# Exponentials in units of three and two PSUM banks, in a kernel whose instruction order a planner writes

## The chip, the core and the metric

The kernel runs on one core of one Trainium2 chip. The metric is the device time of one execution in microseconds; the times shown are of three runs, and the profile is of one further execution on the same chip type.

## What is computed

`x` is 2048 tokens of 512 bf16 values. Block A is attention with 32 heads of 16, block B is an MLP mixer, and a gate mixes both:

```python
def _A_ref(x, wqkv, wo):                    # S = 2048, D = 512, H = 32 heads, Dh = 16
    q, k, v = split(x @ wqkv)
    p = softmax(q @ k.T * Dh ** -0.5)       # 32 x 2048 x 2048 scores
    return (p @ v) @ wo
def _B_ref(x, w1, w2, w3, w4):
    h = gelu(layernorm(x) @ w1)
    hs = shift_quarters(h) @ w2             # quarters of D move by 1, -1, 2, -2 tokens
    x1 = x + hs
    return x1 + gelu(layernorm(x1) @ w3) @ w4      # w3: 512 x 1792
g = sigmoid((x * gate_w).sum(-1))
out = g * _A_ref(x, ...) + (1 - g) * _B_ref(x, ...)
```

The exponentials of 32 x 2048 x 2048 scores are by far the most elements: 2048 tiles of 128 keys by 512 queries (16 blocks of keys, 4 chunks of queries, 32 heads).

## The kernel before

**Rounds and tiles.** Attention goes in 32 rounds (`rounds`): a chunk c of 512 queries, a group G of eight heads, and a parity p that picks four heads of it. A round has 64 score tiles: 16 key blocks (`kt`) times four heads (`i`). One score matmul (`qk_op`, L1313) contracts the 16 values of a head, in a 32-row strip of TensorE, so four heads can run side by side. Queries of the other parity are zeroed by masks `mE` and `mO` (`q_proj`, L1038 and L1040). Each tile fills one PSUM bank of 512 fp32 columns, of which there are eight.

**Two engines make exponentials.** ScalarE takes a unit of `w` tiles in `w` neighbouring banks with one ACTIVATE (`issue_act`, L1408). VectorE takes single tiles by arithmetic on the bits (`issue_dve`, L1439); for each pair of these, VectorE and GpSimd make three shifted copies (L1482, L1484), so that a VectorE tile costs four PV matmuls (L1537) where a ScalarE tile costs one. The results lie in 40 slots of the tile `prob`.

**Column work.** PV matmuls add up in one bank per round (`accs`), 32 output rows of a head each. All projections (Q, K, V, the MLP's four, the output projection) are objects of the class `Gen`: units of four matmuls, one per 32-column strip, that share one bank; VectorE then empties the bank (`evac`). They run through the helper at L964. TensorE changes between score batches (row strips) and column work all the time.

**A planner writes the order.** At build time the class `Sim` models the five engines with fixed durations; `pe_pick` decides at each moment what TensorE does next: first ScalarE units, then VectorE tiles with them, then column work up to the time when a ScalarE unit is expected to end. The result is one fixed instruction order for each queue; SyncE issues nearly all DMAs in one order. What the planner may do is set by the table `BASE`, changed every eight tiles by `STEPS`. What matters here:

- `CAP2` and `CAP3`: the most banks that ScalarE's units may hold when a unit of two or three is added. Before, `CAP3=0` forbids threes until step 253 of 256 (eight tiles a step).
- `GATE`: a ScalarE unit is only started while ScalarE holds at most so many banks.
- `LIMD`, `LIMA`: how many banks VectorE's tiles and projections (`others()`) may hold.
- `DVE_STOP`, `DVE_WAIT`, `DVE_ALONE`, `GP2`, `GP3`, `MAXU`: when VectorE takes tiles, who makes the copies, and how much column work goes in one piece.

```python
            for w, cap in ((3, K.CAP3), (2, K.CAP2)):
                if act_banks[0] + w > cap or free < w + K.RES or not sim.fits(Run("bank", w)):
                    continue
```

**Start and end.** The first two chunks of x are transposed on TensorE (`x_transposes`, L996) and copied out by ScalarE and VectorE (L1006); K of head group 0 for chunk 0 is copied by ScalarE (L1019). After the last PV matmul, the last round's division and output projection follow (L1890 to L1939); `LG` says how many head groups of the last chunk's output projection are added before that.

Of the kernel before, what the change touches and what calls it, by code (L numbers as in the profile page):

```python
# [127 lines left out]
class Gen:  # L128
# [325 lines left out]
def kernel(  # L454
# [14 lines left out]
    nc = tc.nc  # L469
# [12 lines left out]
    LG = 2  # L482
# [45 lines left out]
        ROT=2, DUE_SH=-14, AT_SH=0, HOLE=7, MAXG=1, CAP2=6, CAP3=0, LIMD=3, RES=0, GATE=2, E_PRIO=2, AFIRST=0, AGE=12000, ROWM=99, ACC2=0, LIMA=3, JOIN=0,  # L528
# [3 lines left out]
        0: dict(P1_PRIO=0.743, PV_IDLE=0.5, LIMD=4, E_PRIO=0.25),  # L532
        1: dict(P1_PRIO=0.414, GP2=0.655, PV_IDLE=0.731, MAXU=7, E_PRIO=2, AGE=20000, ROWM=7),
        3: dict(URG=11),
        4: dict(GP2=1, PRESS=43),
        5: dict(DVE_STOP=8),
        6: dict(B_LOW=1),
        8: dict(PV_FULL=0.813, PRESS=26, E_PRIO=0.4),
        9: dict(PV_FULL=0.916),
        11: dict(PV_FULL=0.813, MAXU=2),  # L540
        12: dict(HOLE=2),
        13: dict(S_PRIO=0.178),
        14: dict(AFIRST=1),
        15: dict(SL0=130, HOLE=7),
        16: dict(ROT=3),
        17: dict(URG=3, ROWM=99),
        18: dict(SL0=60),
        21: dict(EARLY=64, B_LOW=5),
        22: dict(DVE_STOP_L=16, ROT=0),
        23: dict(DVE_STOP_L=14, EARLY=99, B_LOW=1, ROT=3),  # L550
        24: dict(AT_SH=69),
        25: dict(PV_FULL=0.916, DUE_SH=-6),
        26: dict(DVE_STOP=13, DVE_WAIT=4, PRESS=15),
        27: dict(P1_PRIO=0.312),
        28: dict(JOIN=1),
        29: dict(AT_SH=34),
        31: dict(E_PRIO=2),
        32: dict(DVE_STOP=8),
        33: dict(P1_PRIO=0.55, GP3=0.9, DVE_STOP=13, DUE_SH=-14, E_PRIO=0.4),
        35: dict(AGE=12000),  # L560
        36: dict(URG=11),
        37: dict(GP2=0.8),
        39: dict(AHEAD=16),
        41: dict(PV_FULL=0.86, PV_IDLE=0.5),
        42: dict(P1_PRIO=0.312),
        43: dict(DVE_STOP=6),
        44: dict(CAP2=5),
        45: dict(B_LOW=0, HOLE=2),
        46: dict(GP3=0.8, ROWM=7),
        47: dict(SL0=-150, AFIRST=0),  # L570
        48: dict(S_PRIO=0.214, SL1=-150),
        49: dict(PRESS=11),
        50: dict(SL1=0, B_LOW=3),
        51: dict(DVE_ALONE=138),
        53: dict(DVE_STOP_L=16, PV_FULL=0.947),
        54: dict(P1_PRIO=0.414, GP2=0.315, GP3=1, DVE_STOP=4, DVE_STOP_L=14, URG=3, DVE_ALONE=500, SL0=45, SL1=-75,
            BRES=2, DVE_WAIT=3, AHEAD=24, AHEAD2=24, PV_IDLE=0.117, PRESS=18, MAXU=9, ROT=0, AT_SH=0, HOLE=3, CAP2=6,
            E_PRIO=2, AFIRST=2, ROWM=99, JOIN=0),
        55: dict(DVE_ALONE=2),
        56: dict(GP2=1, DVE_STOP=13),  # L580
        58: dict(S_PRIO=0.625, AHEAD=16, ROWM=5),
        59: dict(DVE_STOP=6),
        61: dict(SL0=60),
        62: dict(AT_SH=69, AGE=20000),
        63: dict(EARLY=64, BRES=0, HOLE=7),
        64: dict(DVE_STOP=4, PV_IDLE=0.5),
        65: dict(SL0=0),
        66: dict(DVE_WAIT=1),
        67: dict(P1_PRIO=0.136, AT_SH=96, HOLE=2),
        68: dict(P1_PRIO=0.312),  # L590
        69: dict(URG=2, ROT=3),
        70: dict(AGE=12000),
        71: dict(PV_FULL=0.916),
        73: dict(DVE_STOP=8),
        75: dict(DVE_WAIT=2),
        77: dict(S_PRIO=0.214, HOLE=0),
        78: dict(PV_FULL=0.86),
        79: dict(URG=11),
        80: dict(P1_PRIO=0.136),
        81: dict(S_PRIO=0.625),  # L600
        82: dict(AHEAD=5, HOLE=7, ACC2=1),
        83: dict(HOLE=2),
        84: dict(PV_FULL=0.947, ROT=2),
        85: dict(P1_PRIO=0.743, URG_L=18),
        87: dict(ROT=0),
        88: dict(AHEAD=24),
        89: dict(URG=8, AT_SH=69),
        93: dict(S_PRIO=0.178),
        94: dict(GP3=0.8, PV_FULL=0.916, MAXG=2),
        95: dict(DVE_STOP_L=7, ROT=3),  # L610
        97: dict(CAP2=5, AGE=6000),
        98: dict(SL1=0),
        99: dict(ROT=0),
        100: dict(ROT=3),
        101: dict(PV_FULL=0.86, MAXU=5, ROT=0, AT_SH=34, ROWM=99),
        102: dict(S_PRIO=0.625, DVE_WAIT=4, PRESS=11, AGE=3000),
        104: dict(AFIRST=1),
        106: dict(DVE_ALONE=500, AGE=20000, ROWM=5),
        108: dict(ROT=2, LIMA=4),
        109: dict(GP2=0, ROT=3),  # L620
        110: dict(S_PRIO=0.178, URG=2),
        111: dict(GP3=1, AFIRST=0),
        112: dict(P1_PRIO=0.279, S_PRIO=0.214, GP2=1, GP3=0.9, DVE_STOP=4, DVE_STOP_L=16, URG=11, URG_L=12, DVE_ALONE=2,
            EARLY=99, SL0=60, IDLE_NS=374, DVE_WAIT=3, AHEAD=7, PV_FULL=0.947, PV_IDLE=0.117, PRESS=15, MAXU=3, ROT=0,
            DUE_SH=0, AT_SH=0, HOLE=0, MAXG=1, LIMD=3, GATE=4, ROWM=99, ACC2=0, LIMA=3),
        113: dict(P1_PRIO=0.55, S_PRIO=0.178, PV_FULL=0.916),
        114: dict(HOLE=2),
        116: dict(URG=8, DUE_SH=16, MAXG=2),
        117: dict(IDLE_NS=459, B_LOW=8, ACC2=1),
        118: dict(P1_PRIO=0.279, S_PRIO=0.214, URG=11, DVE_ALONE=500, IDLE_NS=374, B_LOW=3, AHEAD=9, PV_FULL=0.947,  # L630
            ROT=1, DUE_SH=0, AT_SH=118, HOLE=7, MAXG=1, ROWM=7, ACC2=0),
        119: dict(PV_FULL=0.813),
        120: dict(DVE_STOP=6, DVE_WAIT=2),
        121: dict(AGE=12000),
        122: dict(GP2=0.315, GP3=1, EARLY=64),
        123: dict(GP2=0.15, PRESS=26),
        124: dict(DVE_STOP=4, DVE_ALONE=-158, EARLY=99, SL0=-75, IDLE_NS=537, DVE_WAIT=3, PV_FULL=0.947, PV_IDLE=0.5,
            PRESS=18, DUE_SH=-9, AT_SH=34, LIMD=4, AGE=20000),
        125: dict(GP2=0),
        126: dict(DVE_STOP_L=12, DUE_SH=0),  # L640
        127: dict(LIMD=3),
        128: dict(DVE_WAIT=4, DUE_SH=-14, ROWM=3),
        129: dict(GP2=0.15),
        130: dict(GP3=0.9, LIMA=2),
        131: dict(MAXU=7, ROWM=7),
        136: dict(P1_PRIO=0.55, URG=5),
        139: dict(P1_PRIO=0.279, URG=11),
        140: dict(ROT=0),
        141: dict(P1_PRIO=0.55, URG=5, ROT=3, AGE=3000, LIMA=3),
        144: dict(P1_PRIO=0.279, URG=11, ROT=1, AGE=20000, LIMA=2),  # L650
        146: dict(URG=2),
        147: dict(PV_FULL=0.86),
        148: dict(ROT=3),
        150: dict(GP3=0.967, URG=11, PV_FULL=0.947, ROT=1),
        151: dict(GP3=0.9, URG=2),
        152: dict(IDLE_NS=374, E_PRIO=0.25, AGE=3000),
        153: dict(GP3=1),
        154: dict(DVE_STOP_L=7, SL1=60, IDLE_NS=700),
        155: dict(PV_FULL=0.86, PRESS=43),
        156: dict(E_PRIO=0.1),  # L660
        158: dict(ROWM=3),
        161: dict(URG=3, ROWM=5),
        163: dict(PV_IDLE=0.731, AGE=12000, LIMA=4),
        164: dict(IDLE_NS=459, PRESS=15, MAXG=2),
        165: dict(S_PRIO=0.178, DUE_SH=0, ACC2=1),
        167: dict(ROT=3),
        168: dict(HOLE=3),
        171: dict(SL1=-75),
        173: dict(HOLE=0),
        174: dict(GP3=0.9),  # L670
        175: dict(P1_PRIO=0.414, S_PRIO=0.38, GP2=1, DVE_STOP=8, DVE_STOP_L=16, URG=8, URG_L=18, DVE_ALONE=2, SL0=0,
            SL1=0, IDLE_NS=537, DVE_WAIT=3, PV_FULL=0.813, PV_IDLE=0.117, PRESS=26, MAXU=5, ROT=1, DUE_SH=-9, AT_SH=96,
            HOLE=7, MAXG=1, CAP2=6, GATE=2, E_PRIO=2, AGE=20000, ROWM=3, ACC2=0, LIMA=2),
        176: dict(URG=11, AT_SH=34, AGE=6000),
        177: dict(ROT=0),
        178: dict(ROT=1),
        179: dict(LIMD=4, E_PRIO=0.4),
        181: dict(ROT=2),
        182: dict(GP3=0.8, MAXU=4),
        183: dict(GP3=0.9, MAXU=5, ROT=1),  # L680
        186: dict(DVE_STOP=6, EARLY=64, AHEAD2=16),
        187: dict(SL1=60, MAXG=2, ACC2=1),
# [1286 lines left out]
```

## Time and profile before

| what | value |
|---|---|
| runs | 756.38, 755.15, 756.24 us, median 756.24 |
| profiled execution | 755.0 us, span 753.0 us, granted clock 0.998 |
| busy: PE, DVE, ACT, POOL | 738.9, 685.8, 732.4, 458.2 us |
| ScalarE exponentials (L1408) | 746 of two banks, 1 of three |
| VectorE exponentials (L1439) | 549 of one bank, 2 of two |
| score matmuls (L1313), PV matmuls (L1537) | 2048, 3707 |
| first exponential starts, last one ends | 10.3 us, 743.9 us after the span's start |

Busy time is the union of an engine's instructions. ScalarE's and TensorE's instructions overlap in the records, so the mean duration of one is longer than the step from one to the next. "PEld" is TensorE's weight load, which runs ahead of the matmul and shows what the matmul waited for.

### The profile page before, as it was taken

How to read it: one execution, taken by the hardware profiler on the slowest of the kernel's cores; microseconds unless marked ns; L12 is line 12 of the kernel's file. 1: busy time of each engine (PE TensorE's matmuls, PEld its weight loads, DVE VectorE, ACT ScalarE, POOL GpSimd, SP SyncE). 2: the span in 40 equal slices, each digit the busy share in tenths (PEclk: the TensorE clock that was granted, in tenths of full speed). 3: DMA queues.
4: the chain of work that ended last, by engine and by line, in shares of the span. 5: the costliest groups of instructions: out<-in, count | busy, mean ns of one | idle time of the engine just before them, and what ended most of it. 6: DMA issues, size and time to landing. Idle time of an engine off the chain costs nothing.

```text
span 753.0 us, 23698 instructions
## 1 busy us (share of the span) xinstructions
PE 738.9 (98%) x9520; PEld 213.2 (28%) x9520; DVE 685.8 (91%) x1422; ACT 732.4 (97%) x768; POOL 458.2 (61%) x456
## 2 busy tenths in 40 slices
PE   8999999999999999998999999999999999999997
PEld 4324322223222222222322222222222223222222
DVE  5999999998999999997999999998989999887897
ACT  6999999999999999998999999999999999999995
POOL 2274686657866676665544545557657877774542
PEclk9999999999999999999999999999999999999999
DMA  9403331221123220025001100012000000101001
GB/s 199 143 4 79 68 85 33 66 66 44 57 61 73 69 55 21 21 72 114 8 24 27 38 26 24 10 30 52 21 20 18 20 6 27 28 24 28 20 7 46
DMA packets 67093, 34.59 MB, mean 46 GB/s; under 512 B 46748, under 2 KB 62380, under 8 KB 66984
## 3 DMA queue, kind: packets, MB, share of 16 engines
q1 hardware_dynamic: 66040, 32.56, 17.0%
q8 instruction: 74, 1.21, 0.7%
q10 hardware_dynamic: 944, 0.52, 0.2%
q14 instruction: 35, 0.29, 0.1%
HBM read 17.40 MB, written 6.81 MB: 32 GB/s over the span
## 4 chain that ended last, share of the span: by engine, by line
PE 85%; DVE 5%; ACT 4%; DMA 4%; issue 1%; POOL 0%; SPq 0%; DVEq 0%; POOLq 0%; ACTq 0%
PE banks L1537 30%; PE banks L1313 29%; PE banks L964 24%; ACT prob L1408 3%; DMA pk<-den 2%; DVE prob L1439 2%; DVE prob L1482 1%; DMA den<-accsb 1%; ACT hT L1218 1%; PE banks L943 0%; DVE st L1122 0%; PE banks L1890 0%; DMA zE_dram<-ot 0%; POOL prob L1484 0%; DMA xnT<-xn_dram 0%
## 5 line engine op out<-in xcount | busy, mean ns | idle before, releaser
L1408 ACT ACTIVATE prob<-banks 128x1024 bf16<-128x1024 f32 (+1 forms) x747 | 687.7, 1143 | 6.3 <-PE banks L1313 5.2
L1484 POOL TENSOR_SCALAR prob<-prob 128x1024 uint16<-128x1024 uint16 x394 | 405.7, 1048 | 255.4 <-DVE prob L1482 108.7
L1439 DVE TENSOR_SCALAR prob<-banks 128x512 uint16<-128x512 f32 x551 | 364.0, 683 | 29.6 <-PE banks L1313 25.6
L1537 PE MATMUL banks<-prob,V 128*17 128x512 bf16 (+1 forms) x3707 | 318.3, 382 | 1.3 <-POOL prob L1484 0.6
L1313 PE MATMUL banks<-q,kT 32*128 32x512 bf16 x2048 | 283.2, 385 | 2.8 <-ACT prob L1408 0.9
L1482 DVE TENSOR_SCALAR prob<-prob 128x1024 uint16<-128x1024 uint16 (+1 forms) x437 | 172.6, 440 | 5.8 <-PE banks L1537 1.7
L1313 PEld LDWEIGHTS <-kT 32*128 32x128 bf16 x2048 | 70.9, 91 | 306.5 <-ACT prob L1408 277.2
L1537 PEld LDWEIGHTS <-V 128*17 128x17 bf16 (+1 forms) x3707 | 71.4, 88 | 122.4 <-issue 102.2
L964 PE MATMUL banks<-xnT,w 128*32 128x512 bf16 x1152 | 91.1, 384 | 3.4 <-DMA xnT<-xn_dram 3.4
L964 PE MATMUL banks<-w,hT 128*32 128x512 bf16 x692 | 63.2, 383 | 0.0
L964 PEld LDWEIGHTS <-w 128*32 128x32 bf16 x1920 | 39.7, 95 | 53.3 <-issue 31.4
L1576 POOL TENSOR_TENSOR oT<-accsb,bcs 128x512 bf16<-128x512 f32 x31 | 39.5, 1275 | 21.0 <-DVE prob L1482 8.4
L964 PE MATMUL banks<-w,hB 128*32 128x512 bf16 x448 | 40.0, 382 | 0.0
L964 PE MATMUL banks<-w,w 128*32 128x256 bf16 (+1 forms) x768 | 38.7, 311 | 0.6 <-DVE V L1063 0.4
L975 PE MATMUL banks<-wo,oD 32*128 32x512 bf16 x72 | 27.7, 384 | 0.0
L1211 DVE CAST hT<-banks 128x512 bf16<-128x512 f32 x28 | 19.1, 682 | 5.2 <-PE banks L964 5.2
L1211 DVE CAST hB<-banks 128x512 bf16<-128x512 f32 x28 | 19.0, 682 | 4.6 <-PE banks L964 4.5
L1558 DVE COPY accsb<-banks 128x512 f32<-128x512 f32 x31 | 21.1, 680 | 1.8 <-PE banks L1537 1.7
L964 PE MATMUL banks<-w,wq 128*32 128x512 bf16 x256 | 21.5, 390 | 0.7 <-ACT w L1006 0.7
L964 PEld LDWEIGHTS <-hT 128*32 128x32 bf16 x692 | 15.9, 95 | 20.3 <-issue 13.7
L1122 DVE BATCH_NORM_STATS2 st<-x_sb 128x6 f32<-128x512 bf16 x32 | 21.1, 678 | 0.0
L964 PE MATMUL banks<-wo,oD 128*32 128x512 bf16 x152 | 20.1, 384 | 0.1
(94 smaller groups left out, 259.1 us busy)
## 6 DMA issues: line engine op xcount, KB each, us to landing
bcs<-rr SPq DMA_DIRECT2D x124, 64.0 KB
xn_dram<-xn SPq DMA_DIRECT2D x32, 128.0 KB
w<-in_B_w_dram SPq DMA_DIRECT2D x5, 512.0 KB
oD<-oT SPq DMA_DIRECT2D x124, 16.0 KB
w<-in_B_w_dram SPq DMA_DIRECT2D x4, 448.0 KB
out_dram<-ot SPq DMA_DIRECT2D x14, 128.0 KB
x_sb<-in_A_x_dram SPq DMA_DIRECT2D x3, 512.0 KB
w<-in_A_wqkv_dram SPq DMA_DIRECT2D x2, 256.0 KB
```

The costliest lines, as they stand in the source:

```text
L964: units.append([Op("col", j, lambda j=j, lf=lf, rf=rf, n0=n0, n1=n1, st=st, sp=sp: nc.tensor.matmul(get()[32 * j:32 * j + 32, n0:n1], lhsT ...
L975: o = Op("row", i, lambda: nc.tensor.matmul(get(), lhsT=lf(0, P)[rows], rhs=rf()[rows], start=False, stop=True, tile_position=(32 * i, 0), ...
L1122: a = dve(600, deps, lambda: nc.vector.bn_stats(out=sb.slot[:], in_=x_sb[:, t, :]), prio=6, at=at, acq=[sb])
L1211: pre.append(evac(g, PSUM_NS, lambda ps, m=m: nc.vector.tensor_copy(out=h2()[:, m, :], in_=ps[:])))
L1313: o = Op("row", i, lambda: nc.tensor.matmul(dst(), lhsT=kT[G][32 * i:32 * i + 32, kt * P:(kt + 1) * P], rhs=qbuf[G, c].slot[32 * i:32 * i ...
L1408: job = act(hold, ops, lambda: nc.scalar.activation(out=prob[:, pb.cut(), :].bitcast(BF16), in_=unit()[:, rb.cut(), :], func=ACT.Exp, scal ...
L1439: return nc.vector.tensor_scalar(out=prob[:, b0.cut() if w == 2 else b0.bufs[h0].slot, :], in0=unit()[:, rb.cut() if w == 2 else rb.bufs[0 ...
L1482: return nc.vector.tensor_scalar(out=cut(k), in0=cut(0), scalar1=float(SHIFT * k), scalar2=None, op0=ALU.add)
L1484: return nc.gpsimd.tensor_scalar(out=cut(k), in0=cut(0 if both else 2), scalar1=1.0, scalar2=float(SHIFT * (k if both else 1)), op0=ALU.mu ...
L1537: return nc.tensor.matmul(one(accs[r])[32 * i:32 * i + n, :], lhsT=lhs(n), rhs=rhs(), start=st and not edge, stop=True, tile_position=(0, ...
L1558: e = dve(PSUM_NS, round_ops[r], lambda: nc.vector.tensor_copy(out=ab.slot[:], in_=one(accs[r])), acq=[ab], prio=0, frees=[accs[r], Call(a ...
L1576: n = gp(1250, d3, lambda: nc.gpsimd.tensor_tensor(out=ob.slot[:], in0=ab.slot[:], in1=bb.slot[:], op=ALU.mult), acq=[ob], frees=[ab, bb], ...
```

## The change

ScalarE's units may have three banks from the start: `CAP3=5`, and `CAP2` goes from 6 to 5, so ScalarE holds five banks at most, and a unit of three is tried ahead of one of two. `GATE` is 4, 2, 3 or 9 by stages. The whole table `STEPS` is replaced. Besides:

- A projection's input buffers are given back by the matmul that is issued last, not by the one whose strip completes the last unit.
- Chunk 0 is transposed block by block, each in a bank of its own; K of group 0 for chunk 0 is made in two halves (`k_first`), and tiles of its first two key blocks may start after the first half; the first masked queries are written half by VectorE, half by ScalarE; chunk 1's transposes and V's projection wait for that (`begun`), and chunk 1's copies are all VectorE's.
- The planner's durations are changed (ns): loads of transposed x from 3100 to 3500, writes of `xn_dram` from 2200 to 2600, loads of `xnT` from 3000 to 3600, of `pk` from 2000 to 2800, of `bcs` from 2200 to 3000; around a Gelu 3050 becomes 3450 in the first layer and 2750 in the second.
- `LG` is 3 rather than 2; at the end the fp32 additions (`add_y`) come first, and the output projection of the known groups may start earlier if its inputs are expected in time.

```diff
@@ Gen.take
-        if min(self.cp) == self.cp[j]:
-            for x in self.units[k]:
-                if x is not o:
-                    o.frees += x.frees
-                    x.frees = []
+        rest = [i for i in range(4) if self.cp[i] < self.cp[j]]
+        if rest:
+            self.units[k][rest[-1]].frees += o.frees
+            o.frees = []
@@ settings
-    LG = 2
+    LG = 3
-        ROT=2, DUE_SH=-14, AT_SH=0, HOLE=7, MAXG=1, CAP2=6, CAP3=0, LIMD=3, RES=0, GATE=2, E_PRIO=2, AFIRST=0, AGE=12000, ROWM=99, ACC2=0, LIMA=3, JOIN=0,
+        ROT=2, DUE_SH=-14, AT_SH=0, HOLE=7, MAXG=1, CAP2=5, CAP3=5, LIMD=3, RES=0, GATE=2, E_PRIO=2, AFIRST=0, AGE=9000, ROWM=99, ACC2=0, LIMA=3, JOIN=0,
     STEPS = {
-        0: dict(P1_PRIO=0.743, PV_IDLE=0.5, LIMD=4, E_PRIO=0.25),
-        1: dict(P1_PRIO=0.414, GP2=0.655, PV_IDLE=0.731, MAXU=7, E_PRIO=2, AGE=20000, ROWM=7),
...
+        0: dict(GP2=1, URG=8, B_LOW=8, DVE_WAIT=1, PV_IDLE=0.5, GATE=4, AFIRST=2),
+        1: dict(SL1=130, AT_SH=34),
...
+        28: dict(DVE_WAIT=2),
+        30: dict(DVE_WAIT=1, PRESS=18, GATE=3),
...
+        41: dict(MAXU=2, GATE=9, LIMA=4),
...
+        62: dict(DUE_SH=-9, GATE=3, LIMA=2),
...
+        249: dict(GP2=0.15, DUE_SH=16, GATE=9),
@@ x_transposes: one call for each block of chunk 0
-    x_transposes(0, 0, j_x0)
-    x_transposes(0, 1, j_x0)
-    k_proj(0, 0, -1)
+    for k in range(KT):
+        x_transposes(0, (k,), j_x0)
+    k_first()
     q_proj(0, 0, -1)
-    x_transposes(1, 0, j_x1)
-    x_transposes(1, 1, j_x1)
+    begun = [j_ka[0], j_q[0, 0, 0]]
+    x_transposes(1, (0, 2), j_x1 + begun)
+    x_transposes(1, (1, 3), j_x1 + begun)
@@ who copies the transposed blocks
-            j_xT[c, 0, k] = (dve if k % 2 else act)(340 if k % 2 else 500, g.units[k // 2], cp, prio=0, frees=[g.buf])
+            on_dve = c or k % 2
+            j_xT[c, 0, k] = (dve if on_dve else act)(375 if on_dve else 535, g.units[n], cp, prio=0, frees=[g.buf])
@@ new
+    def k_first():
+        for h in range(2):
+            g = gen("k0", -1, [j_xT[0, 0, k] for k in range(KT)] + [dl_w["k0"]],
+                    [(lambda a, b, k=k: W("k")[:, k, a:b],
+                      lambda k=k, h=h: W("x00")[:, k, 256 * h:256 * h + 256], 0, 256, k == 0, k == KT - 1, 107.5)
+                     for k in range(KT)], due=-3 + h)
+            if h:
+                g.ops[-1].frees += [wb["k"], wb["x00"]]
+            j = act(275, g.units[-1], lambda g=g, h=h: nc.scalar.copy(out=kT[0][:, 256 * h:256 * h + 256],
+                                                                      in_=one(g.buf)[:, 0:256]), prio=0, frees=[g.buf])
+            if h:
+                j_k[0, 0] = j
+            else:
+                j_ka.append(j)
@@ q_proj, first block only
-            e1 = dve(680, g.units[-1] + [j_m3], lambda: nc.vector.tensor_scalar(
-                out=qb.slot[:, 0, :], in0=one(g.buf)[:], scalar1=mE[:], scalar2=None, op0=ALU.mult), prio=0, acq=[qb])
+            e1 = [dve(345, g.units[-1] + [j_m3], lambda: nc.vector.tensor_scalar(
+                out=qb.slot[:, 0, 0:256], in0=one(g.buf)[:, 0:256], scalar1=mE[:], scalar2=None, op0=ALU.mult), prio=0,
+                acq=[qb])]
+            e1.append(act(330, g.units[-1] + [j_m3], lambda: nc.scalar.activation(
+                out=qb.slot[:, 0, 256:512], in_=one(g.buf)[:, 256:512], func=ACT.Copy, scale=mE[:]), prio=0))
@@ tile_ok
+        k = j_ka[0] if G == 0 and kt < 2 else j_k.get((G, kt // 4))
@@ room
-        return sim.free["bank"] and others() < K.LIMD
+        return sim.free["bank"] and others() < (K.LIMD if sim.tiles else NBANK)
@@ end
-    early = (0, 1) if max(d.done for d in packs) < tl - 500.0 else ()
+    early = (0, 1) if max(d.done for d in packs) < tl + 1500.0 else ()
...
-    for tt in range(4):
-        if tt not in early:
-            known(tt, range(LG, 3))
-    add_y(1)
-    add_y(3)
+    for tt in (1, 3):
+        add_y(tt, tt not in early)
     for tt in range(4):
         if tt not in early:
-            known(tt, (3,))
+            known(tt, range(LG, 4), tt % 2 == 0)
```

More of the change, by code (lines that the diff above doesn't have):

```diff
@@ new lines @@
+        1: dict(SL1=130, AT_SH=34),
+        2: dict(DUE_SH=-9),
+        3: dict(SL0=130),
+        4: dict(AHEAD=5, AT_SH=69),
+        6: dict(URG=3),
+        7: dict(SL1=60),
+        8: dict(S_PRIO=0.178, PRESS=57),
+        9: dict(E_PRIO=0.1),
+        10: dict(P1_PRIO=0.279),
+        11: dict(P1_PRIO=0.414),
+        13: dict(P1_PRIO=0.136),
+        14: dict(URG=8, PV_FULL=0.97),
+        16: dict(GP3=0.8, IDLE_NS=864, AGE=20000),
+        21: dict(MAXU=3),
+        22: dict(URG_L=18, AT_SH=118),
@@ new lines @@
+        68: dict(ROT=2),
+        70: dict(ROT=3, AFIRST=2, LIMA=2, JOIN=0),
+        71: dict(GP3=1),
+        74: dict(URG=11),
+        75: dict(GP3=0.8, URG=2),
+        76: dict(AT_SH=96),
+        77: dict(URG=5, AHEAD=12),
+        78: dict(URG=3),
+        83: dict(DVE_STOP=6),
+        84: dict(B_LOW=3, ROT=0),
+        85: dict(GP3=1),
+        86: dict(GP3=0.8),
+        88: dict(AT_SH=34),
+        89: dict(P1_PRIO=0.414, GP2=0.315, ACC2=0),
+        90: dict(P1_PRIO=0.136, GP2=0.15, DVE_ALONE=500, PRESS=26, ACC2=1),
@@ new lines @@
+        93: dict(DVE_STOP=8, URG=8),
+        94: dict(PV_FULL=0.813, PV_IDLE=0.5),
+        95: dict(DVE_STOP=6, URG=3, PV_FULL=0.97, PV_IDLE=0.117, PRESS=8),
+        96: dict(GP3=0.967),
+        98: dict(SL0=-75, AGE=12000),
+        100: dict(SL1=-150),
+        101: dict(SL1=-75, IDLE_NS=374, HOLE=2),
+        102: dict(AFIRST=0),
+        103: dict(MAXU=4),
+        104: dict(MAXU=5),
+        105: dict(SL0=-150),
+        106: dict(GP3=0.8, LIMA=4),
+        107: dict(URG_L=12, MAXU=2),
@@ new lines @@
+        108: dict(URG_L=18, MAXU=5),
+        109: dict(ACC2=0),
+        111: dict(URG_L=12, MAXU=2, ACC2=1),
+        112: dict(BRES=4, AHEAD=7, PRESS=15, JOIN=1),
+        114: dict(GP2=0.315),
+        115: dict(SL1=0, BRES=0),
+        116: dict(GP2=1, URG=2, EARLY=99),
+        118: dict(GP2=0.655),
+        119: dict(SL1=130),
+        120: dict(GP2=0.15, DVE_STOP_L=12, MAXU=7),
+        121: dict(SL0=0, AT_SH=118),
+        122: dict(HOLE=0, JOIN=0),
+        124: dict(B_LOW=5, ROT=2, AGE=3000),
@@ new lines @@
+        125: dict(PRESS=26),
+        126: dict(HOLE=7),
+        128: dict(DVE_STOP=8, PV_FULL=0.813),
+        129: dict(GP3=0.967, EARLY=64, IDLE_NS=459),
+        130: dict(GP3=0.8, ROWM=3),
+        132: dict(PRESS=18),
+        133: dict(PV_FULL=0.947, DUE_SH=-14),
+        134: dict(GP3=0.633),
+        135: dict(GP3=0.8),
+        136: dict(ROWM=99),
+        137: dict(GP3=0.9, AHEAD2=16, ACC2=0),
+        138: dict(AHEAD=24),
+        142: dict(GP2=0.8),
+        143: dict(GP3=1, PRESS=11),
@@ new lines @@
+        146: dict(AGE=12000),
+        147: dict(GP3=0.9, PRESS=18, AGE=3000),
+        150: dict(GP2=1, ACC2=1),
+        152: dict(GP2=0.8, ACC2=0),
+        153: dict(HOLE=0),
+        154: dict(S_PRIO=0.3, DVE_STOP_L=14),
+        155: dict(S_PRIO=0.178, DVE_STOP_L=12),
+        156: dict(ROWM=7),
+        157: dict(HOLE=7),
+        158: dict(P1_PRIO=0.743, GP3=0.967, B_LOW=0, DVE_WAIT=3),
+        159: dict(P1_PRIO=0.136, DVE_STOP=6, URG=3),
+        162: dict(DVE_WAIT=1, ROWM=3),
+        166: dict(AFIRST=2),
@@ new lines @@
+        185: dict(ROT=3),
+        186: dict(SL1=130, ROT=2, AT_SH=69, E_PRIO=2),
+        187: dict(SL1=60, DVE_WAIT=4, ROT=3, AT_SH=0, E_PRIO=0.1),
+        188: dict(P1_PRIO=0.414, DVE_STOP=13, B_LOW=2, MAXG=1),
+        189: dict(MAXU=3),
+        191: dict(AGE=20000, ACC2=1),
+        192: dict(DVE_STOP=6),
+        193: dict(ROT=1),
+        194: dict(ROT=3),
+        195: dict(PRESS=26),
+        196: dict(PRESS=18, ROT=1),
+        197: dict(DVE_STOP=8, PRESS=43),
+        198: dict(DVE_STOP=6, URG=8, PRESS=18),
@@ new lines @@
+        200: dict(DVE_STOP=4),
+        201: dict(URG_L=18, AHEAD=3, AFIRST=0),
+        202: dict(DVE_ALONE=362),
+        203: dict(GP2=0),
+        204: dict(P1_PRIO=0.279),
+        205: dict(P1_PRIO=0.414, GP2=0.8, DVE_ALONE=500, ROWM=7),
+        208: dict(P1_PRIO=0.136),
+        209: dict(SL0=0, HOLE=3),
+        210: dict(AT_SH=69),
+        212: dict(GP2=0.15),
+        213: dict(HOLE=0),
+        214: dict(AGE=3000),
+        215: dict(AGE=20000),
+        216: dict(SL0=130, B_LOW=0),
@@ new lines @@
+        218: dict(SL0=0, B_LOW=2, AGE=3000),
+        219: dict(GP3=0.9, IDLE_NS=374),
+        220: dict(AT_SH=0),
+        221: dict(GP3=0.967, ROT=3),
+        223: dict(GP2=0.8, URG_L=12, AGE=12000),
+        224: dict(SL0=-75, AGE=6000),
+        228: dict(AGE=3000),
+        230: dict(ACC2=0),
+        231: dict(DVE_STOP_L=16, SL1=130, PV_FULL=0.86),
+        232: dict(P1_PRIO=0.279),
+        234: dict(GP3=0.9),
+        235: dict(URG=5, B_LOW=3),
+        238: dict(URG=8, DVE_ALONE=362, B_LOW=1),
@@ L905, in load_xT @@
     def load_xT(c, k, part, prio):
-        return dma(3100.0, [], lambda: xT_dma(c, part, k)(nc.sync), hold=1280.0, prio=prio,
+        return dma(3500.0, [], lambda: xT_dma(c, part, k)(nc.sync), hold=1280.0, prio=prio,
                    acq=[wb[f"x{c}{part}"]] if k == 0 else [])
@@ L1016, in k_proj @@
         g.ops[-1].frees += [wb["k"], wb[f"x{c}0"]]
-        if G == 0 and c == 0:
-            g.due = -3
-            j_k[G, c] = act(500, g.units[-1], lambda: nc.scalar.copy(out=kT[G][:, 0:512], in_=one(g.buf)[:]), prio=0,
-                            frees=[g.buf])
-            return
-        g.due = 14 * c - 6 if G == 0 else g.due
+        g.due = 14 * c - 11 if G == 0 else g.due
         j_k[G, c] = evac(g, PSUM_NS, lambda ps: nc.vector.tensor_copy(out=kT[G][:, c * 512:(c + 1) * 512], in_=ps[:]),
@@ L1057, in v_proj @@
         c = u // 2
-        g = gen("v", at, [j_xT[c, 0, k] for k in range(KT)] + [dl_w[f"v{hh}"]],
+        g = gen("v", at, begun + [j_xT[c, 0, k] for k in range(KT)] + [dl_w[f"v{hh}"]],
                 [(lambda a, b, t=t, k=k: W(f"x{c}0")[:, k, (t % 4) * P + a:(t % 4) * P + b],
@@ L1151, in normalise @@
         for k in range(KT):
[L1152 removed]
+            js.append(dma(3600.0, ds, hold=1280.0, fn=lambda k=k: nc.sync.dma_start(
                 out=tb.slot[:, k, :], in_=xn_dram[which, c * 512:(c + 1) * 512, k * P:(k + 1) * P], transpose=True),
@@ L1307, in tile_ok @@
         c, G, p = rounds[r]
-        return ready_round(r) and j_k.get((G, kt // 4)) is not None and j_k[G, kt // 4].done is not None
+        k = j_ka[0] if G == 0 and kt < 2 else j_k.get((G, kt // 4))
+        return ready_round(r) and k is not None and k.done is not None
     def qk_op(r, kt, i, dst, buf, lat):
```

290 lines of the change are left out of this document (69 added, 221 removed).

## The prediction

> **What bounds the kernel now.** I read the page's busy shares first, then the groups by line and form, the timeline, and last the list of waits.
>
> ```profile
> PE 738.9 (98%) x9520; PEld 213.2 (28%) x9520; DVE 685.8 (91%) x1422; ACT 732.4 (97%) x768; POOL 458.2 (61%) x456
> ```
>
> Three engines look full, and the chain that ended last is 85% PE. PE's figure says least, because its ends are modelled and its instructions overlap. The groups tell who does the 2048 score tiles of 128x512:
>
> ```profile
> L1408 ACT ACTIVATE prob<-banks 128x1024 bf16<-128x1024 f32 x746 | 686.5, 1142 | 6.3 <-PE banks L1313 5.2 <-POOL prob L1484 0.7
> ...
> L1439 DVE TENSOR_SCALAR prob<-banks 128x512 uint16<-128x512 f32 x549 | 361.6, 681 | 29.0 <-PE banks L1313 25.1 <-POOL prob L1484 0.3 <-PE banks L1537 0.3
> ...
> L1482 DVE TENSOR_SCALAR prob<-prob 128x1024 uint16<-128x1024 uint16 x434 | 172.0, 441 | 5.8 <-PE banks L1537 1.7 <-POOL prob L1484 1.0 <-ACT prob L1408 0.7
> ...
> L1408 ACT ACTIVATE prob<-banks 128x1536 bf16<-128x1536 f32 x1 | 1.5, 1488 | 0.0
> ```
>
> ScalarE takes 746 pairs and one unit of three: 1495 tiles. VectorE takes the other 553 (549, and two instructions of two). ScalarE's instructions overlap, so 1142 ns is not the pace. ScalarE's timeline gives it:
>
> ```profile
> 47.33 18.41 ACT L1408 ACTIVATE prob<-banks 128x1024 bf16<-128x1024 f32 x20
> ...
> 740.59 3.32 ACT L1408 ACTIVATE prob<-banks 128x1536 bf16<-128x1536 f32 x3
> ```
>
> Twenty pairs in 18.41 us, less the last one's own 1.14, over 19 steps is 0.91; the trace's start times put it at 0.904 us, the shortest of 746 steps and also their median. The second row is the unit of three and two pairs: 3.32 less one step of 0.904 and the last one's 1.087 leaves 1.33 (1.331 by the starts). So a bank costs 1331 - 904 = 427 ns, and an instruction 904 - 854 = 50 ns. The stretch between the first and the last exponential, as the view by windows has it:
>
> ```profile
> core 0: us, PE busy (x) PEld busy (x) DVE busy (x) ACT busy (x) POOL busy (x), PEclk, DMA share, GB/s
> 10.30:743.90 733.60, 725.47 (x9366) 206.53 (x9366) 678.18 (x1405) 726.98 (x759) 454.28 (x442) 1.00 0.17 44
> ```
>
> And the waits (who waited for whom: us in total, times, longest):
>
> ```profile
> PEld L1313 <- ACT prob L1408: 277.2, 641, 0.6
> ...
> DVE prob L1439 <- PE banks L1313: 25.6, 74, 1.1
> ...
> DVE pk L1565 <- DMA pk<-den: 4.4, 5, 1.3
> ...
> PE banks L964 <- DMA xnT<-xn_dram: 3.4, 2, 2.5
> ```
>
> From its first exponential (10.3) to the end of its last (743.9) ScalarE has 733.6 us. Of these 746 x 0.904 + 1.331 = 675.7 are units at full pace; 39.4 are Gelus (7.0 at L1181, 12.4 and 12.3 at L1218) and six table loads of 1.28; 18.5 are left, of which steps longer than the pace make 13.9. The first wait says that PE's score matmuls (L1313) waited 641 times for ScalarE to give banks back: ScalarE sets the pace, PE follows closely. The timeline shows how closely:
>
> ```profile
> 300.33 0.39 PE L1313 MATMUL banks<-q,kT 32*128 32x512 bf16 x3
> ...
> 300.65 0.62 PE L964 MATMUL banks<-xnT,w 128*32 128x512 bf16 x8
> ...
> 300.88 0.62 DVE L1439 TENSOR_SCALAR prob<-banks 128x512 uint16<-128x512 f32 x1
> ...
> 301.19 0.39 PE L1313 MATMUL banks<-q,kT 32*128 32x512 bf16 x3
> ```
>
> A score batch costs PE 0.32 us until the next column matmul starts, eight column matmuls 0.54: 0.86 us in a ScalarE step of 0.904.
>
> **The change, part by part**, against the profiled execution's own 755.0 us (span 753.0 and 2.0 around it). The median of the runs is 756.24, so 1.2 is added at the end.
>
> *Units of three and two.* Strict alternation does 1495 banks in 598 instructions. At ends of rounds and around Gelus only two tiles or banks may be free, so I take 610. That removes 137 x 50 ns = 6.9 us from the engine that sets the pace, all of it on the path. Bounds: 0 (no threes) to 7.5.
>
> The Trainium skill, "ScalarE: Activation LUTs", section "What ACT_TABLE_LOAD costs", gives an ACTIVATE with immediate operands 186 ns besides its elements and an overlap of 93 ns back to back, so 93 ns per instruction. By it this term would be 12.7 us and the total, an estimate, 739.7; the trace's 50 ns decides.
>
> *Does PE keep up?* While the two runs (0.904) the three freed banks must be refilled, and while the three runs (1.331) the two. The first is the tight case and as tight as today's: a unit's recorded end is 0.24 after the next one's start (1142 - 904), the weight load follows 0.06 later, and in the head a first exponential starts 0.43 after its first score matmul (9.86, 10.29): 0.73 of 0.904. In the second case there is 0.43 more room. For column work five banks give 2.235 us: 8 matmuls beside the short unit, 16 beside the long (0.32 and an estimated 4 x 0.22 + 0.10 make 1.30 of 1.331), 24 in all; three pairs take 2.71 for those 24. So PE is relieved, and I book nothing for it, because PE waits for ScalarE already.
>
> *Waits.* The planner's DMA and copy durations are raised; its row order moves so that PE and VectorE find their data (the 3.4 and 4.4 above). No DMA is added or taken away, but SP is one queue in order: each transfer issued later delays those behind it. The tables of settings are all new, so small waits fall elsewhere. Of the 13.9 I take 2 away; bounds 6 less to 8 more.
>
> *Tiles to VectorE.* The split comes out of the planner, and no row shows the new one. One tile moved costs or saves ScalarE 0.447 us ((1.331 + 0.904)/5). I keep 553; 12 tiles either way are 5 us, the rivals hold the rest.
>
> *Head.* Now the copies at L1006 start at 5.56, after eight transposes that share a bank; ScalarE then copies kT (8.65 to 9.24) and two blocks of the next chunk (9.19 to 10.26), and only then comes the first exponential, 10.29, though scores began at 9.86. After: a bank for each block (last copy done near 6.4, not 6.77), masks of the first half split over both engines (0.75 becomes about 0.42), half of k copied first, the next chunk's copies on VectorE and behind the start. Step by step: query projection 6.35, masks 7.5 to 7.95, half of kT to 8.35, scores 8.42, exponential 8.85. That is 1.4; I take 1.2, bounds 0 and 1.5. V's projection and chunk 1's transposes now wait for this start; behind them on PE are only the first PV matmuls, and 40 prob slots let these wait.
>
> *Tail.* The output projection's group 2 moves before the last round (LG 3): 16 of 48 matmuls at L1890 go. VectorE's first half of oT is ready at 746.90, yet L1932 starts at 747.77 behind them; 16 at 0.054 are 0.86. I take 0.6, bounds 0.3 worse to 1.2; if the moved work stalled on its packing DMAs, the next to be late would be PE in the last round.
>
> *Buffers given back by the last issued matmul:* nothing; the xnT wait covers it, 3.4 us if it were all wrong or all cured.
>
> Sum: -6.9 - 2.0 - 1.2 - 0.6 = -10.7: 744.3, as a median 745.5.
>
> **Rivals.**
>
> *1. Banks run short for VectorE: slower.* ScalarE holds two units, one being read and one refilled: four of eight banks now, five after; the accumulator holds one; three left become two. A VectorE tile holds a bank from 300.33 to 301.50, 1.17 us: 553 of them 647 us, 0.86 bank. A projection holds one from 300.65 to the end of its cast at 303.52, 2.87 us; some 150 casts and adds make 431 us, 0.57 bank. That is 1.43 of 2, where it was 1.43 of 3. It fits on average; when both are taken, VectorE waits (the 25.6 us now). It decides once VectorE does over 24 tiles fewer (10.7/0.447), below 529. At 500, ScalarE gets 53 x 0.447 = 23.7 more: 755.0 - 10.7 + 23.7 + 1.2 = 769. For it: a VectorE tile goes with a score batch, so a bank must be free at that very moment, and ScalarE is served first. Against: banks free sooner when PE has spare time.
>
> The Trainium skill, "TensorEngine Tiling (Array Packing)", section "Gotcha 1: PSUM Pressure", has row tiles raise the pressure on PSUM since each writes its own bank, which is this rival's ground. The trace agrees so far as the batch of three at 300.33 fills a ScalarE pair of 1024 columns and a VectorE tile of 512.
>
> *2. VectorE takes more.* PE's relief allows it: a VectorE tile adds three PV matmuls. VectorE is idle 753.0 - 685.8 = 67.2 us and a tile costs it (361.6 + 172.0)/553 = 0.965. Half of the idle time is 35 tiles, 15.6 us off ScalarE: 730. Against: the banks of rival 1.
>
> *3. Threes are rarely found.* A unit of three needs three neighbouring banks, three row groups and three evenly spaced prob slots, or the planner falls back on two. Then head and tail alone remain: 755.0 - 1.8 + 1.2 = 754.4.
>
> **Chances and range.** Forecast 0.55, rival 1 0.20, rival 2 0.15, rival 3 0.10. About 0.2%, 1.5 us, is what a measurement of this kernel can tell from no change; rival 3 lies on that edge and is split. So faster 0.75, same 0.06, slower 0.19. The forecast's own range is 737 to 753 (waits, and 12 tiles either way). With the milder halves of rivals 1 and 2, and rival 3, it is 733 to 763.
>
> **What would show it.** Right: about 610 exponentials, over 250 of them 128x1536; first one near 9.1; from the last one's end to the span's end about 8.5 instead of 9.1; VectorE's tiles at L1439 within 12 of 553; L1313 still waiting mostly for ScalarE. Rival 1: fewer tiles at L1439 and its wait for L1313 well over 25.6. Rival 2: 580 tiles or more and VectorE above 94%. Rival 3: pairs in the majority. Wrong altogether: ScalarE's idle time before L1408 above 20 us, so that PE sets the pace.

## The result, and the profile after

The changed kernel takes 765.22 us (median of 4 runs, 764.22 to 766.92), the kernel before 756.31 on the same chip: ratio 1.0106, 95% interval 1.0076 to 1.0136. It is slower by 8 to 9 us, and its time lies 2 us above the predicted range. The profiled execution took 764.97 us, span 763.2, against 755.0 and 753.0.

The page's first line, and the groups by line and form (line numbers have moved: L1399 is ScalarE's exponential, L1430 VectorE's, L1473 VectorE's shifted copies, L1304 the score matmul):

```profile
PE 742.8 (97%) x9323; PEld 226.6 (30%) x9323; DVE 664.5 (87%) x1381; ACT 746.2 (98%) x642; POOL 362.4 (47%) x362
```

```profile
L1399 ACT ACTIVATE prob<-banks 128x1536 bf16<-128x1536 f32 x308 | 499.3, 1621 | 1.6 <-PE banks L1528 1.1 <-PE banks L1304 0.5
L1399 ACT ACTIVATE prob<-banks 128x1024 bf16<-128x1024 f32 x313 | 373.0, 1193 | 3.0 <-PE banks L1528 1.6 <-PE banks L1304 1.3
L1430 DVE TENSOR_SCALAR prob<-banks 128x512 uint16<-128x512 f32 x498 | 337.5, 686 | 63.2 <-PE banks L1304 57.0 <-POOL prob L1475 1.1 <-ACT prob L1399 1.0
...
L1473 DVE TENSOR_SCALAR prob<-prob 128x1024 uint16<-128x1024 uint16 x447 | 183.3, 445 | 7.3 <-PE banks L1528 2.5
```

The change does what it says: 308 units of three and 313 of two. But these hold 1550 tiles where ScalarE had 1495, because VectorE's went from 553 to 498. ScalarE is busier than before (746 us), VectorE less (87% after 91%) and GpSimd far less (47% after 61%). VectorE now sits idle for 57.0 us until score matmuls have filled a bank for it, where it was 25.6.

ScalarE's timeline confirms the pace:

```profile
99.78 10.50 ACT L1399 ACTIVATE prob<-banks 128x1536 bf16<-128x1536 f32 x9
```

Nine units that alternate, a three first and last: 4 x (1.331 + 0.904) = 8.94 up to the last one's start, which leaves 1.56 for the last. No time is lost between units. The view by windows has the stretch between the first and the last exponential:

```profile
core 0: us, PE busy (x) PEld busy (x) DVE busy (x) ACT busy (x) POOL busy (x), PEclk, DMA share, GB/s
8.60:754.50 745.90, 731.79 (x9196) 220.47 (x9197) 657.74 (x1366) 741.31 (x633) 358.55 (x348) 1.00 0.17 43
```

With the prediction's own terms the 10.2 us of span come apart like this (us; "rest" is the stretch less units at full pace less 39.4 for Gelus and table loads):

| term | before | after | difference |
|---|---|---|---|
| tiles on ScalarE x 0.427 | 1495: 638.4 | 1550: 661.9 | +23.5 |
| instructions x 0.050 | 747: 37.3 | 621: 31.0 | -6.3 |
| rest (waits) | 18.5 | 13.6 | -4.9 |
| start to first exponential | 10.29 | 8.64 | -1.65 |
| last exponential's end to the end | 9.11 | 8.68 | -0.43 |

The terms by which the change was to gain are all there, 13.3 us in all. The tiles that came over from VectorE cost 23.5. The fall of the rest need not come from the threes: below, c_two4_7banks has no threes, and its rest falls too when VectorE does fewer tiles.

The waits show the new shortage. Before, then after:

```profile
PEld L1313 <- DVE prob L1439: 3.3, 9, 0.4
...
PEld L964 <- DVE prob L1439: 2.9, 12, 0.4
```

```profile
PEld L1304 <- ACT prob L1399: 240.4, 550, 0.9
...
DVE prob L1430 <- PE banks L1304: 57.0, 107, 2.8
...
PEld L1304 <- DVE prob L1430: 17.2, 40, 0.5
...
PEld L937 <- DVE prob L1430: 8.7, 34, 0.4
```

VectorE waits for PE to fill a bank, and PE waits 74 times for VectorE to give one back (L1304 and the projections at L937), where it was 21 times: both wait for the same few banks. One such place in the timeline:

```profile
311.71 0.09 PEld L1304 LDWEIGHTS <-kT 32*128 32x128 bf16 x1 [0.43 <-DVE prob L1430]
311.71 0.87 PE L1304 MATMUL banks<-q,kT 32*128 32x512 bf16 x4
...
312.19 0.10 PEld L1304 LDWEIGHTS <-kT 32*128 32x128 bf16 x3 [0.39 <-ACT prob L1399]
312.23 0.68 DVE L1430 TENSOR_SCALAR prob<-banks 128x512 uint16<-128x512 f32 x1
```

At 311.71 one score matmul alone goes for VectorE, as soon as VectorE has freed a bank; half a microsecond later the next batch goes, three matmuls for ScalarE's freed banks. Two batches where one served both at 300.33 in the kernel before.

The bank numbers are in the program, and each engine runs its instructions in the program's order, so every score matmul and projection in the trace can be paired with the instruction that empties its bank. A bank is counted from the start of the first matmul into it to the end of the last read. Between ScalarE's first and last exponential this gives:

| mean number of banks held by | before | after |
|---|---|---|
| ScalarE's units | 3.84 | 4.71 |
| VectorE's tiles | 1.28 | 0.91 |
| projections | 0.89 | 0.72 |
| VectorE's tiles and projections together | 2.17 | 1.63 |

Before, VectorE's tiles and projections held three banks or more for 36% of this time. Two banks can't give the 2.17 that they used; after the change two or more are held for 61% of the time.

### The profile page after: what moved, and what is told of

Its sections match the earlier page's. It is cut to its first block, busy times and chain, and to the rows that moved or that the text cites. A ratio compares the mean times of both kernels' runs of the same rounds, so it can differ in the third digit from the quotient of the medians.

```text
span 763.2 us, 22981 instructions
## 1 busy us (share of the span) xinstructions
PE 742.8 (97%) x9323; PEld 226.6 (30%) x9323; DVE 664.5 (87%) x1381; ACT 746.2 (98%) x642; POOL 362.4 (47%) x362
## 4 chain that ended last, share of the span: by engine, by line
PE 61%; ACT 26%; DVE 7%; issue 4%; DMA 1%; POOL 1%; DVEq 0%; ACTq 0%; POOLq 0%
ACT prob L1399 25%; PE banks L1304 21%; PE banks L1528 21%; PE banks L937 18%; DVE prob L1430 2%; DVE prob L1473 2%; DMA xn_dram<-xn 1%; DVE st L1112 1%; POOL prob L1475 1%; PE banks L916 0%; DVE V L1053 0%; DVE accsb L1549 0%; PE banks L968 0%; DVE kT L1009 0%; ACT L1399 0%
## 5 line engine op out<-in xcount | busy, mean ns | idle before, releaser
L1399 ACT ACTIVATE prob<-banks 128x1536 bf16<-128x1536 f32 (+1 forms) x621 | 702.1, 1405 | 4.6 <-PE banks L1528 2.8
L1475 POOL TENSOR_SCALAR prob<-prob 128x1024 uint16<-128x1024 uint16 x300 | 309.7, 1045 | 354.9 <-DVE prob L1473 150.2
L1430 DVE TENSOR_SCALAR prob<-banks 128x512 uint16<-128x512 f32 x498 | 337.5, 686 | 63.2 <-PE banks L1304 57.0
L1528 PE MATMUL banks<-prob,V 128*17 128x512 bf16 (+1 forms) x3542 | 305.9, 382 | 0.7 <-DVE prob L1430 0.7
L1304 PE MATMUL banks<-q,kT 32*128 32x512 bf16 x2048 | 288.9, 385 | 13.7 <-ACT prob L1399 6.9
L1473 DVE TENSOR_SCALAR prob<-prob 128x1024 uint16<-128x1024 uint16 x447 | 183.3, 445 | 7.3 <-PE banks L1528 2.5
L1304 PEld LDWEIGHTS <-kT 32*128 32x128 bf16 x2048 | 74.7, 91 | 300.7 <-ACT prob L1399 240.4
L1528 PEld LDWEIGHTS <-V 128*17 128x17 bf16 (+1 forms) x3542 | 74.6, 89 | 129.6 <-issue 97.1
L937 PE MATMUL banks<-xnT,w 128*32 128x512 bf16 x1152 | 89.3, 383 | 0.0
L937 PEld LDWEIGHTS <-w 128*32 128x32 bf16 x1936 | 42.4, 95 | 47.4 <-issue 25.9
L1567 POOL TENSOR_TENSOR oT<-accsb,bcs 128x512 bf16<-128x512 f32 x31 | 39.4, 1272 | 28.9 <-DVE prob L1473 20.0
L937 PE MATMUL banks<-w,hT 128*32 128x512 bf16 x692 | 52.7, 383 | 0.0
L937 PE MATMUL banks<-w,w 128*32 128x256 bf16 (+1 forms) x784 | 39.1, 312 | 0.2
L937 PE MATMUL banks<-w,hB 128*32 128x512 bf16 x448 | 31.9, 382 | 0.1
L937 PE MATMUL banks<-wo,oD 128*32 128x512 bf16 x220 | 21.5, 382 | 0.0
L937 PEld LDWEIGHTS <-hT 128*32 128x32 bf16 x692 | 14.4, 95 | 20.4 <-issue 11.9
L937 PE MATMUL banks<-w,wq 128*32 128x512 bf16 x256 | 18.8, 383 | 0.0
L1132 DVE TENSOR_SCALAR xn<-x_sb,rs,nm 128x512 bf16<-128x512 bf16 x32 | 12.1, 405 | 3.0 <-DMA xn_dram<-xn 3.0
```

Of the source, the lines that this page charges most:

```text
L937: units.append([Op("col", j, lambda j=j, lf=lf, rf=rf, n0=n0, n1=n1, st=st, sp=sp: nc.tensor.matmul(get()[32 * j:32 * j + 32, n0:n1], lhsT ...
L1132: g = dve(323, [m], lambda t=t, xb=xb: nc.vector.tensor_scalar(out=xb.slot[:], in0=x_sb[:, t, :], scalar1=rs[which][:, t:t + 1], scalar2=n ...
L1304: o = Op("row", i, lambda: nc.tensor.matmul(dst(), lhsT=kT[G][32 * i:32 * i + 32, kt * P:(kt + 1) * P], rhs=qbuf[G, c].slot[32 * i:32 * i ...
L1399: job = act(hold, ops, lambda: nc.scalar.activation(out=prob[:, pb.cut(), :].bitcast(BF16), in_=unit()[:, rb.cut(), :], func=ACT.Exp, scal ...
L1430: return nc.vector.tensor_scalar(out=prob[:, b0.cut() if w == 2 else b0.bufs[h0].slot, :], in0=unit()[:, rb.cut() if w == 2 else rb.bufs[0 ...
L1473: return nc.vector.tensor_scalar(out=cut(k), in0=cut(0), scalar1=float(SHIFT * k), scalar2=None, op0=ALU.add)
```

## Experiments

Two theories were to be told apart. **Banks**: VectorE takes as many tiles as it gets banks, and five banks for ScalarE leave two where there were three. **Table**: the new settings table gives VectorE less, and the widths are innocent. Variants of each (VectorE's own time; the unit of three as such) go with the runs. How many tiles VectorE has is fixed when the program is built, so the expectations give that number; the run tells the time and the waits.

### Four bank counts, no table

The changed kernel's code, one constant setting, four splits of the banks:

```diff
+    STEPS = {}
+    BASE.update(CAP2=4, CAP3=0, GATE=2, GP2=0.3, GP3=0.9)     # c_two4
+    BASE.update(CAP2=5, CAP3=5, GATE=4, GP2=0.3, GP3=0.9)     # c_three5
+    BASE.update(CAP2=4, CAP3=0, GATE=2, GP2=0.3, GP3=0.9)     # c_two4_7banks, with
-    NBANK = 8
+    NBANK = 7
+    BASE.update(CAP2=6, CAP3=0, GATE=4, GP2=0.3, GP3=0.9)     # c_two6
```

> Changed kernel's code with one constant setting in place of the table (GP2=0.3, GP3=0.9), ScalarE in units of two, four banks at most, so three banks are left for VectorE's tiles and projections. This and the next three kernels have the same settings and differ in banks alone. Theory 'banks' (the number of banks left to VectorE sets how many tiles it takes): the program gives VectorE the most of the four, 544. Theory 'table' (the new table gives VectorE less, banks are innocent): without a table all four would give about the same number. Time, either theory: PE has the most batches per tile and the plan is untuned, so well over 755; about 780.

> Same constant setting, units of three and two, five banks at most: two banks left. Banks: about a hundred tiles fewer than with two4 (the program has 441), so 103 x 0.447 = 46 us more work for ScalarE, of which its shorter overhead (about 110 instructions x 0.05) and PE's relief give back a part; slower than two4 by 5 to 30 us, VectorE's wait for score matmuls (L1304) clearly longer. Table: no slower than two4, since the threes save instructions.

> Same constant setting, units of two, four banks at most, but the planner is given seven banks instead of eight: two left, as with threes, without threes. Banks: VectorE's number falls to about that of three5 (the program has 460), and the time is longer than two4 by 10 to 30 us and not shorter than three5, since there is no saving from threes. Rival 'shape' (it is the units of three as such, for instance that they need three neighbours and three row strips): number and time stay near two4's.

> Same constant setting, units of two, but six banks at most: one bank left for VectorE and projections together. Banks: VectorE's number falls once more (the program has 382) and the kernel is the slowest of the four by far, over 840, because ScalarE gets 1666 tiles and projections block VectorE. Shape: like two4.

| kernel | banks left besides ScalarE's and the accumulator's | VectorE tiles | VectorE's wait for score matmuls | time |
|---|---|---|---|---|
| c_two4 | 3 | 544 | 26.5 | 782.5 |
| c_three5 | 2 | 441 | 97.1 | 797.5 |
| c_two4_7banks | 2 | 460 | 95.3 | 802.3 |
| c_two6 | 1 | 382 | 126.0 | 879.5 |

The waits of c_two4, c_three5 and c_two4_7banks, in this order:

```profile
DVE prob L1432 <- PE banks L1306: 26.5, 65, 1.3
```

```profile
DVE prob L1432 <- PE banks L1306: 97.1, 167, 1.7
```

```profile
DVE prob L1432 <- PE banks L1306: 95.3, 155, 1.5
```

And of c_two6:

```profile
DVE prob L1432 <- PE banks L1306: 126.0, 184, 2.4
```

Taking one bank away from units of two does to VectorE's wait what units of three do, within 2 us, and gives nearly the same number of tiles. So it is the bank count, not the three as a shape. The threes' own worth shows between the two kernels that leave two banks: c_three5 is 4.8 us faster than c_two4_7banks, with 19 VectorE tiles fewer. Both are far behind c_two4. Each of these kernels was run once, and the differences of 15 and 20 us are many times the spread of runs.

The loss is only about half of what the moved tiles cost. ScalarE's units at full pace are 679.8 us in c_two4, 718.3 in c_three5 and 717.8 in c_two4_7banks, 38 us more; but the rest falls from 43.8 us to 20.6 and 24.4. A price by the tiles alone is too high where ScalarE has waits to lose.

### Is it the table, or VectorE's time?

The changed kernel with one of its settings forced through the whole table, or its widths put back; and the old table with threes (one run each):

```diff
+    for d in STEPS.values():            # the key is taken out of every step first
+        ...
+    BASE.update(DVE_WAIT=3)                    # a_wait3: changed kernel
+    BASE.update(GP2=1, GP3=1)                  # a_gp: changed kernel
+    BASE.update(CAP2=6, CAP3=0, GATE=2)        # a_two: changed kernel
+    BASE.update(CAP2=5, CAP3=5, GATE=4)        # b_three: kernel before
```

> Changed kernel with one setting forced through its whole table: DVE_WAIT=3, so up to three score tiles may wait for VectorE, as in the kernel before; its table mostly allows one, later four. Table theory: this limit is why VectorE took 498; with it lifted the number rises toward 553. Banks theory: no bank is there for a second waiting tile, so the number doesn't rise above 510 (the program has 491). The rest of the table was fitted to the old order, so the time is longer either way, by 10 to 45 us, and says little.

> Changed kernel with GP2=1 and GP3=1 through the whole table: GpSimd makes two of the three shifted copies wherever it may, so VectorE has some 60 us less to do. Theory 'VectorE's time' (the new table gives VectorE more copies, 447 for 498 tiles instead of 437 for 553, and that is what crowded out tiles): the number of tiles rises above 520. Banks: VectorE's time isn't what is short, the number stays at or below 498 (the program has 484) and VectorE's busy share falls below 82%. Time longer, 10 to 30 us, since the table was fitted to another order.

> Changed kernel, its own table, but units of two only (CAP3=0, CAP2=6, GATE=2: normally four banks). Banks: VectorE's tiles go up from 498 although the table is the same (the program has 534). Table theory: they stay near 498. Time: the table was fitted to threes, so it is longer than the changed kernel's either way, 780 to 810; PE waits more often and the steps of ScalarE beyond its pace add up to 40 us or more.

> Kernel before, its own table, but with units of three and two and five banks (CAP2=5, CAP3=5, GATE=4). Banks: VectorE's tiles fall from 553 by 50 or more (the program has 445) with the table unchanged. Table theory: they stay near 553. Time, by 445 tiles: ScalarE's units 318 x 1.331 + 324 x 0.904 = 716, which is 40 us more than before, so 780 to 800.

Letting more tiles wait for VectorE gives it 491 instead of 498, at 809.0 us. Taking copies off it leaves it with 484, at 792.5:

```profile
PE 763.3 (97%) x9377; PEld 236.7 (30%) x9377; DVE 627.6 (79%) x1189; ACT 755.4 (96%) x648; POOL 522.8 (66%) x518
```

VectorE is down to 79% and waits 80.6 us for score matmuls: it has time and no banks. With the widths exchanged the numbers follow the widths, whichever table: the new table with twos 534 (802.5 us, VectorE's wait down to 26.8), the old one with threes 445 (805.9, just above what I expected; wait 101.0). The waits of a_two and b_three:

```profile
DVE prob L1434 <- PE banks L1308: 26.8, 54, 1.4
```

```profile
DVE prob L1443 <- PE banks L1317: 101.0, 163, 1.5
```

Not all of the 55 tiles are shown to be the widths' doing: with the new table, units of two bring back 36 of them, and what takes the other 19 was not separated. The times of these four say little by themselves, since a table fits the order for which it was found: in a_two the rest of ScalarE's stretch is 59.9 us, in b_three 27.9, against 18.5 and 13.6 in the two kernels with tables of their own.

### A table of its own for each width

To be fair to both widths, each got a table from the same search in the changed kernel's code: at each of 256 stages 60 random changes of settings, each planned 40 stages ahead and the best by the planner kept.

```diff
+    BASE.update(CAP2=6, CAP3=0, GATE=2, GP2=0.3, GP3=0.9, ...)   # s_two
+    STEPS = {0: dict(GP2=0.315), 2: dict(ACC2=1, DVE_STOP=6), ...}          # 152 steps
+    BASE.update(CAP2=5, CAP3=5, GATE=4, GP2=0.3, GP3=0.9, ...)   # s_three
+    STEPS = {0: dict(DUE_SH=-14, MAXU=9, AT_SH=118, DVE_WAIT=2), ...}       # 156 steps
```

> Changed kernel's code with a table found anew for units of two (up to six banks, the GATE setting decides; normally four): at each of the 256 stages 60 random changes of the settings are tried in the planner for 40 stages ahead, and the best is kept. The same search, of the same size and from the same start, is made for threes in s_three. Theory 'banks': even with a table of its own, two leaves VectorE more tiles (the program has 526) and is the faster of the two; time about 757 to 765, against the kernel before, whose table is the product of much more search. Theory 'table' (the changed kernel is slow only because its table is poorer than the old one, the widths don't matter): s_two and s_three come out within 4 us of each other.

> The same search, same size, same start, for units of three and two with five banks (the program has 467 VectorE tiles, 316 units of three and as many of two). Banks: slower than s_two by 8 to 20 us, with ScalarE's units at full pace 316 x (1.331 + 0.904) = 706 us against 761 x 0.904 = 688 for two. Table: within 4 us of s_two.

s_two: 762.07 us, 1.0043 of before (1.0027 to 1.0058). s_three: 782.43, 1.0316 (1.0286 to 1.0345). Threes lose by 20 us, at the upper end of what the bank theory gave, and not within 4. The groups of s_two and of s_three:

```profile
L1585 DVE TENSOR_SCALAR prob<-banks 128x512 uint16<-128x512 f32 x524 | 347.6, 682 | 46.9 <-PE banks L1459 37.7 <-POOL prob L1630 2.2 <-PE banks L1683 1.4
```

```profile
L1589 DVE TENSOR_SCALAR prob<-banks 128x512 uint16<-128x512 f32 x467 | 315.8, 685 | 74.6 <-PE banks L1463 69.0 <-PE banks L1687 1.7
```

VectorE's tiles are 526 (524, and one instruction of two) and 467; ScalarE's units at full pace 687.9 and 706.7 us, which is 18.8 of the 21.1 us between the spans (761.0 and 782.1). With the small search, twos already beat the changed kernel (1.0043 of before against 1.0106; the ratios are compared, since the two ran on different chips). The table matters too, on its own: the changed kernel has the same widths as s_three and is about 16 us faster by the ratios, with 31 VectorE tiles more. Why the changed kernel lost only 8 us to the old one, where s_three loses 20 to s_two, I read from this: its table is a much better one. How far a still longer search would bring threes was not tried.

### Two small parts alone

```diff
     # b_frees: kernel before, Gen.take as in the change
+        rest = [i for i in range(4) if self.cp[i] < self.cp[j]]
+        if rest:
+            self.units[k][rest[-1]].frees += o.frees
+            o.frees = []
     # b_tail: kernel before, the end as in the change
-    LG = 2
+    LG = 3
...
+    for tt in (1, 3):
+        add_y(tt, tt not in early)
```

> Kernel before with its own table and units of two; the only edit is that a projection's inputs are given back by its last issued matmul. I had booked nothing for it. If that is right the time stays within 3 us of the kernel before. Theory 'fitted table': a buffer that comes free at another moment changes the planner's order from that point on, the old table no longer fits it, and the kernel is 5 to 15 us slower with about as many VectorE tiles (the program has 544).

> Kernel before with its own table and units of two, and of the change only the end: LG=3 and the new order after the last PV matmul. This is the one part of the change that leaves the old order alone but for its last stages (the program has 551 VectorE tiles). By the prediction's term the stretch from the last exponential's end to the span's end falls by 0.6 us, from 9.1 to 8.5, and the kernel is 0 to 1 us faster than before, the best of all so far by a margin near what can be measured. Rival 'fitted table': the few tiles that the new order moves in the last round cost as much as the end gains, and the time is the same or up to 3 us longer.

b_frees: 765.64 us, 1.0094 (1.0064 to 1.0125). An edit for which I had booked nothing costs the old table about as much as the whole change costs: VectorE's tiles go to 544, the rest of ScalarE's stretch to 25.3 us. With a table of its own it may cost less; that was not run, so its price apart from the table is not known.

b_tail: 0.9994 (0.9979 to 1.0010), no difference that can be told. The end itself went from 9.11 to 8.39 us, as the term said, and the last exponential ended 0.5 later. In its profile the first exponential starts at 9.78, where the kernel before, with the same start, has 10.29: one profile's head is good to about 0.5 us. No version beat the kernel before by more than can be measured.

## Why the prediction was wrong

*The pace* (904 and 1331 ns, 50 ns for an instruction) held: the medians over the 621 units are the same to 1 ns. *Units of three and two*: 126 instructions fewer instead of 137, 6.3 us instead of 6.9. The Trainium skill's 93 ns for an instruction ("ScalarE: Activation LUTs", "What ACT_TABLE_LOAD costs") would have asked for steps of an estimated 946 and 1373 ns; the trace's are 904 and 1331.

*PE keeps up*: right. ScalarE's idle time before its exponentials is 4.6 us.

*Waits*: the rest fell by 4.9 us where I took 2. In the trace of the kernel before, all steps beyond the pace add up to 17.0 us, not to 13.9; the 2 that I took hang on neither.

*Head and tail*: 1.65 and 0.43 instead of 1.2 and 0.6. One step of the head was wrong: the two halves of the query mask do not run side by side. VectorE writes its half at 6.89 and ScalarE starts the other at 7.41, released by VectorE:

```profile
6.89 0.48 DVE L1024 TENSOR_SCALAR q<-banks,mE 128x256 bf16<-128x256 f32 x1 [0.76 <-PE banks L937]
7.41 0.47 ACT L1027 ACTIVATE q<-banks,mE 128x256 bf16<-128x256 f32 x1 [1.30 <-DVE q L1024]
```

The two take 0.99 us where one instruction took 0.75 before; I had 0.42. The copies were earlier than I had them (the query projection starts at 5.68, not 6.35), which more than made up for it.

*Tiles to VectorE*: this is the step that failed. I kept 553 and booked 0; it was 498, and the 55 tiles cost ScalarE 55 x 0.427 = 23.5 us (24.6 at the 0.447 that I gave per tile with its share of instructions). I had the mechanism as rival 1, with the place (three banks left become two), the deciding point (below 529 tiles) and a price, 769 at 500 tiles; measured was 765.2 at 498, lower mainly because the waits shrank by 2.9 us more than I took. I gave it 0.20.

What misled me is the sentence "It fits on average". I counted one VectorE tile that was taken from its bank almost at once, 1.17 us, and one projection, 2.87 us, and set 1.43 banks against two. In the trace of the kernel before, a VectorE tile holds its bank for 1.10 us at the least and for 1.70 on average, because VectorE is mostly still busy when the tile is ready (it waited for a score matmul 74 times for 551 instructions); with the projections that makes the 2.17 banks of the table above, more than two. So it didn't fit even on average. After the change the mean is 1.36 us: now VectorE waits for tiles instead. There is also the moment: a VectorE tile needs its bank at a score batch, and these come every 0.9 or 1.3 us; a bank that comes free a little later waits for the next batch, or costs one of its own as at 311.71.

The Trainium skill, "TensorEngine Tiling (Array Packing)", section "Gotcha 1: PSUM Pressure", says that row tiling raises the pressure on PSUM, which pointed this way. What a bank is worth the runs here say: one bank fewer costs 20 us (c_two4_7banks), and six for ScalarE cost 97 (c_two6).

*Frees*: "nothing" was wrong as a price of its own (b_frees, 0.9% or about 7 us with the old table). Inside the change, whose table was made with it, its part was not measured apart.

## What to carry to other kernels

When engines share a buffer pool and split work by whoever is free, price a wider unit on one by what the others take with the buffers that are left: here 13 us of gains were outweighed by 55 tiles that changed hands. Take how long a buffer is held as a mean over the whole trace, not from one place where all went well. Test such a claim by taking one buffer away without the change; if the loss is the same, it is the buffer. And where an order was searched for, an edit's time includes the order's fit: compare widths with tables of the same effort, or with none.

## What the runs showed of the hardware

Little that was not expected. The two halves of the query mask are read from one PSUM bank and written to one tile, and the program as built makes the second engine wait for the first (6.89, then 7.41), so the split between two engines took the sum of both times here, 0.99 us. Whether the chip would bear both at once was not tried.
